# An S4D convolution by FFT: the input's 4096-point spectrum and the way back split as 128 by 32 instead of 64 by 64

## The chip, the cores and the metric

The kernel runs on one core of a Trainium2 chip. The metric is device time in microseconds (us), from start to end of one execution. The core's engines are TensorE (PE; its weight loads are listed apart as PEld), VectorE (DVE), ScalarE (ACT), GpSimd (POOL) and SyncE (SP), whose queue issues nearly all of the transfers. Matmuls read SBUF and write PSUM, which has eight banks of 2 KB per partition.

## The reference

The block takes `A_u` of 2048 tokens by 448 channels, normalizes and modulates it, convolves each channel with a kernel of length 2048 that is a sum of 256 damped complex exponentials, adds the result to the input, and puts a token-mixing MLP (2048 to 1792 to 2048 tokens) behind it.

```python
h = layernorm(x) * (1 + ca) + sa
K = 2 * Re(einsum("dn,dnl->dl", C, exp(A * dt * pos)))      # 448 channels, 2048 positions
y = irfft(rfft(h, 4096) * rfft(K, 4096))[:2048]             # linear convolution
x = x + ga * (y + h * D_skip)
h = layernorm(x) * (1 + cb) + sb
x = x + gb * (W2 gelu(W1 h^T + b1) + b2)^T                  # MLP over tokens
```

## The kernel before

**Stages.** The program has a first part (span 0 to about 390 us) that makes the convolution, and a second (to the end) with the layer norms and the MLP. The first part is one loop over steps s = 0 to 58 that generates the convolution kernel K in 28 groups of 16 channels, two steps for each group. The spectral work is laid between the steps. A "window" stands at every eighth step: it makes the magnitudes (exponentials) of the next eight steps.

**A step.** `st_phase` puts angles into PSUM by matmuls (`xe`, `xg`, line 627). `st_step` runs six ACT functions of 512 columns (lines 683 to 688), two POOL products `G` (690, 691) and four DVE products `E` (692 to 696). `st_mag2` makes a magnitude product on POOL (666, 671), in the loop for later steps below 32 and in the windows otherwise. `st_kgen` sums E times G over the exponentials on PE (`kg`, 717). `st_s1` transforms a finished pair of groups along one axis (`y`, 755, 32 matmuls of 64x64 into two PSUM tiles), and two copies put it into `yk` (761).

**The spectrum of the input.** The transform has 4096 points, split 64 by 64. `u_rows` (548; 32 calls) multiplies a quarter of the partitions (32 tokens) by a row table `wur`, which POOL makes from `wu` and the layer norm's scales (535). The result goes through `yt` to DRAM (`yu_d`). `u_cols` (580; 32 calls, k = 0 to 31) loads it as `yi`, multiplies one row by a 128x128 column table out of `s2`, and adds a constant term on DVE (587) for the 17 rows in `ones_k1`; for the other 15 rows ACT copies (589). Two rows go to `us_d` in one transfer. Rows are dealt out two or three per step in steps 8 to 16, columns two or three per step in steps 17 to 28 and one per turn in the window at step 24.

**The pieces.** 16 pairs of rows times two halves of 224 channels are 32 pieces. For each, `pc_s2` makes the spectrum of the kernel (`kx`, 820: two 128x128 matmuls of 224 columns), `pc_mul` multiplies by the input's spectrum (`z`, 828, two on DVE), `pc_inv` transforms back (`vv`, 836 and 837: four matmuls of 128x128), `pc_out` copies to `vt` (842) and stores to `v_d` (846). Pieces 0 to 15 stand inside the loop from step 33, one operation group per step, with a table of 384 KB each (`si`). Pieces 16 to 31 stand behind the loop, one after another. There `pc_swap` makes a copy of `u` with its halves exchanged (805, ACT), and `pc_tables` makes a third of the tables on POOL out of the two thirds that are loaded (811 to 813). The MLP's first part, `ln_y`, ends the way back by the 32-point table `ft` (1308).

**What sets the order.** PE, ACT, DVE and POOL run in the order in which the code calls them; results that leave PSUM are put on the lists `dve` and `act`, which are emptied in the middle of the next `st_step` and after its ACT functions, or at each turn of a window. SP's queue is ordered by hand in part of the program and elsewhere by the framework. PSUM tiles of `u_rows`, `u_cols`, `y`, `kx` and `vv` come from the pool `pms` with three banks, taken in turn; behind the loop `kx` has the pool `pxs` with four.

Of the kernel before, what the change touches and what calls it, by code (L numbers as in the profile page):

```python
# [22 lines left out]
P = 128  # L23
# [17 lines left out]

def dft_tables():
    n1 = np.arange(32)
    k1 = np.arange(32)
    n2 = np.arange(64)
    k2 = np.arange(64)
    nn = 4096
    t = {}
    w = 2 * np.pi * np.outer(n1, k1) / 64
# [9 lines left out]
    t["WU"] = np.tile(w1.transpose(1, 2, 0).reshape(32, 64), (4, 1))  # L59

    t["WC"] = wc.reshape(P, 2, 2, 2, 32).swapaxes(3, 4).reshape(P, 2 * P)
    s = np.zeros((2, 64, 32, 2, 64))
    i1 = np.zeros((2, 64, 32, 2, 64))
    i2 = np.zeros((2, 64, 32, 2, 64))

    def inverse(rows, cols, k, m, ang):
        a = np.cos(ang) * 2 / nn
        b = np.sin(ang) * 2 / nn
        i1[0, rows, k, m[0]] = a
        i1[1, rows, k, m[0]] = -b  # L70
        i2[1, rows, k, m[0]] = -a
        i2[0, rows, k, m[0]] = -b
        if len(m) > 1:
            i1[0, rows, k, m[1]] = b
            i1[1, rows, k, m[1]] = a
            i2[1, rows, k, m[1]] = -b
            i2[0, rows, k, m[1]] = a

    for k in range(1, 32):
        ang = 2 * np.pi * np.outer(n2, k + 64 * k2) / nn  # L80
        s[0, :, k, 0] = np.cos(ang)
        s[1, :, k, 0] = np.sin(ang)
        s[0, :, k, 1] = -np.sin(ang)
        s[1, :, k, 1] = np.cos(ang)
        inverse(slice(None), None, k, (0, 1), ang.T)


    for q in range(32):
        ang = 2 * np.pi * n2 * (32 + 64 * q) / nn
        s[1, :, 0, 0, q] = np.cos(ang)  # L90
        s[1, :, 0, 1, q] = -np.sin(ang)
        inverse(q, None, 0, (1,), ang)
    for q in range(33, 64):
        ang = 2 * np.pi * n2 * (64 * (q - 32)) / nn
        s[0, :, 0, 0, q] = np.cos(ang)
        s[0, :, 0, 1, q] = -np.sin(ang)
        inverse(q, None, 0, (0,), ang)
    s[0, :, 0, 0, 32] = 1
    s[0, :, 0, 1, 32] = (-1.0) ** n2
    i1[0, 32, 0, 0] = 1 / nn  # L100
    i2[1, 32, 0, 0] = (-1.0) ** n2 / nn
    s2 = s.reshape(P, 32 * P)

    t["S2"] = s.reshape(2, 4, 8, 2, 32 * P).transpose(3, 0, 2, 1, 4).reshape(P, 32 * P)

    one = np.einsum("cnk,cqkm->km", w1, s.reshape(2, 64, 32, P))
    t["SV"] = one[ones_k1()].T

    order = lambda a: a.reshape(P, 32, 2, 2, 2, 16).transpose(0, 1, 5, 2, 4, 3)
    t["I1"] = order(i1)  # L110
    t["I2"] = order(i2)
    ft = np.zeros((32, 2, 2, 32, 2))
    w = 2 * np.pi * np.outer(k1, n1) / 64
    f0 = np.cos(w)
    f1 = -np.sin(w)
    f0[0] = 1
    f1[0] = (-1.0) ** n1
    for h in range(2):
        ft[:, 0, h, :, h] = f0
        ft[:, 1, h, :, h] = f1  # L120
    t["FT"] = ft.reshape(P, 64)
    fl = np.zeros((4, 4, 2, 2, 2 * LAST, 2, 64))
    for r in range(2):
        for g in range(2):
            fl[r, :, g, r, :, g] = t["FT"].reshape(32, 4, 64)[-2 * LAST :].swapaxes(0, 1)
    t["FL"] = fl.reshape(32, 2 * 2 * LAST * P)
# [16 lines left out]

    v1, v2 = (t.pop(k).reshape(2, 64, 32, P) for k in ("I1", "I2"))
    j1 = np.stack([v1[0], v2[1]])
    j2 = np.stack([v1[1], v2[0]])
    for nm, tabs, n in (("SI", (s2, v1, v2), NP), ("SJ", (s2, j1, j2), 1), ("SK", (s2, v1), NP)):
        tabs = [a.reshape(P, NP, 2, P)[:, :n] for a in tabs]  # L150
        t[nm] = np.stack(tabs, 2).reshape(P, n * len(tabs) * 2 * P)
    return {k: np.ascontiguousarray(v.astype(np.float32)) for k, v in t.items()}


def ones_k1():

    return [0] + list(range(1, 32, 2))


def token_rows(a):  # L160

    return a.rearrange("(n g h r) d -> r g n h d", g=2, h=2, r=16)


def token_pair(a, r, g):

    rows = a.rearrange("(n g h r) d -> g n h (r d)", g=2, h=2, r=16)
    return rows[g, :, :, r * D : (r + 2) * D]


class WeightStream:
# [12 lines left out]
    def load(self):  # L184
# [4 lines left out]
        if n < 32:  # L189
            fh, r = divmod(n, 16)  # L190
            for g in range(2):
                self.nc.sync.dma_start(w[64 * g : 64 * g + 64], self.w1[r, g, :, :, fh * 896 : (fh + 1) * 896])
# [34 lines left out]
def tile_adaln_s4d_mixer(ctx, tc, i, out):  # L227
    nc = tc.nc
    x = i["A_u"][0]
    xv = x.rearrange("(n g r) d -> r g n d", g=4, r=16)  # L230
# [17 lines left out]
    with ExitStack() as es:  # L248
# [54 lines left out]
        def x_load(r0, n, eng=nc.sync):  # L303
            for g in range(4):
                to = xt[32 * g : 32 * g + 32, r0 : r0 + n, 0:D]
                (nc.sync if r0 > 7 and g < 2 else eng).dma_start(to, x.rearrange("(n g r) d -> g n r d", g=4, r=16)[g, :, r0 : r0 + n])
# [19 lines left out]
        wu = xp.tile([P, 64], F32, name="wu")  # L326
# [7 lines left out]
        svt = sp2.tile([P, 17], F32, name="svt", bufs=1)  # L334
# [197 lines left out]
        def u_table(R):  # L532
            wurs[R] = xp.tile([P, 2, 64], F32, tag="wur", name="wur", bufs=3)
# [39 lines left out]
        def u_cols(k):  # L573
# [22 lines left out]
            if k % 2 and k // 2 + 4 < 16:  # L596
                u_load(k // 2 + 4)
                if kk == 3 and n + 2 < 8:
                    s2_load(n + 2)
# [868 lines left out]
```

## Time and profile before

| | |
|---|---|
| three timed runs | 694.22, 697.17, 698.87 us; median 697.17 |
| the profiled execution | 692.88 us; span 691.1 us, mean granted clock of TensorE 0.988 |
| busy, of the span | PE 642.3, PEld 485.7, ACT 451.0, DVE 429.0, POOL 277.0 us |
| transfers | 128.15 MB in 99759 packets, mean 185 GB/s |
| from 500 us on | PE 25.0 of every 25 us, MLP only |

The profile counts the busy time of an engine as the union of its instructions. A busy sum by group (an instruction's line, its tiles, its shape) adds overlapping instructions, so PE groups add up to more than the span. One f32 matmul is two records. DMA shares are of the 16 DMA engines and go up to 1.08 where all of them are always at work.

### The profile page before, as it was taken

To read this page: it belongs to the slowest core of one execution; us is meant where nothing else is said; L and a number is where in the kernel's file an instruction comes from. 1 tells how busy PE (TensorE), PEld (TensorE's weight loads), DVE (VectorE), ACT (ScalarE), POOL (GpSimd) and SP (SyncE) were. 2 spreads that over 40 slices of the span, in tenths; PEclk is the share of its full clock that TensorE was granted. 3 is DMA by queue.
4 is the path that set the end of the run, shared out by engine and by line. 5 is a ranking of instruction groups with operands and counts; after the bars stand their busy time and mean duration, and the time that the engine had idled before them with its cause. 6 is when DMAs were issued, how large, how long until landed. Compare 5 with 4: busy or idle time off the path is not lost.

```text
span 691.1 us, 18518 instructions
## 1 busy us (share of the span) xinstructions
PE 642.3 (93%) x7322; PEld 485.7 (70%) x7322; DVE 429.0 (62%) x818; ACT 451.0 (65%) x848; POOL 277.0 (40%) x363
## 2 busy tenths in 40 slices
PE   0877999999988899999999989999999999999997
PEld 0444555445445676676789857778899999999997
DVE  7896899786665584856744578876732364444431
ACT  5788598899869799999767678887322352222220
POOL 6685588498578767777658200000000000000000
PEclk9989999999999899999999999999999999999999
DMA  7695757598876476554589799955563445555540
GB/s 180 183 204 139 241 172 239 205 253 245 242 231 168 124 171 162 143 162 122 142 266 375 227 263 246 250 151 153 180 215 113 141 133 160 160 167 168 166 125 28
DMA packets 99759, 128.15 MB, mean 185 GB/s; under 512 B 13460, under 2 KB 80440, under 8 KB 99672
## 3 DMA queue, kind: packets, MB, share of 16 engines
q1 hardware_dynamic: 98728, 124.34, 63.4%
q0 software_dynamic: 944, 2.62, 1.6%
q8 instruction: 58, 0.95, 0.6%
q14 instruction: 29, 0.24, 0.1%
HBM read 91.57 MB, written 34.87 MB: 183 GB/s over the span
## 4 chain that ended last, share of the span: by engine, by line
PE 69%; DMA 10%; ACT 8%; DVE 5%; issue 3%; POOL 2%; SPq 1%; DVEq 0%; ACTq 0%; POOLq 0%
PE o L1434 7%; PE o L1436 6%; PE o L1435 6%; PE xe L627 6%; PE acc L1271 6%; PE acc L1272 6%; PE acc L1273 5%; PE kg L717 5%; PE vv L836 3%; PE vv L837 3%; PE kx L820 3%; DMA w<-in_B_w_dram 3%; PE pu L580 3%; PE pu L548 2%; DMA wm<-in_w_mod_dram 2%
## 5 line engine op out<-in xcount | busy, mean ns | idle before, releaser
L212 ACT CAST whi<-w 128x896 fp32r<-128x896 f32 x64 | 59.7, 939 | 135.1 <-PE o L1435 82.6
L690 POOL TENSOR_TENSOR G<-mag,gs 128x512 f32<-128x512 f32 x56 | 72.0, 1286 | 52.4 <-ACT gs L686 52.4
L221 DVE TENSOR_TENSOR wlo<-w,whi 128x896 fp32r<-128x896 f32 x64 | 68.1, 1086 | 39.6 <-ACT whi L212 36.5
L1271 PE MATMUL acc<-h3h,whi 128*128 128x448 f32 x224 | 83.0, 371 | 2.0 <-ACT h3h L1344 1.1
L1272 PE MATMUL acc<-h3l,whi 128*128 128x448 f32 x224 | 81.3, 363 | 0.6 <-DVE h3l L1345 0.4
L1434 PE MATMUL o<-uh,whi 128*128 128x448 f32 x224 | 81.3, 363 | 0.0
L1436 PE MATMUL o<-uh,wlo 128*128 128x448 f32 x224 | 81.2, 362 | 0.0
L1273 PE MATMUL acc<-h3h,wlo 128*128 128x448 f32 x224 | 80.9, 361 | 0.0
L1435 PE MATMUL o<-ul,whi 128*128 128x448 f32 x224 | 80.6, 360 | 0.0
L717 PEld LDWEIGHTS kg<-E,G 128*32 128x32 f32 x3584 | 55.9, 113 | 29.3 <-issue 18.5
L691 POOL TENSOR_TENSOR G<-mag,gs 128x512 f32<-128x512 f32 x56 | 72.0, 1286 | 0.0
L717 PE MATMUL kg<-E,G 128*32 128x64 f32 x3584 | 65.2, 226 | 3.2 <-issue 2.6
L627 PE MATMUL xg<-tab,lph 64*128 64x512 f32 x112 | 62.6, 559 | 5.1 <-DVE E L696 2.0
L627 PE MATMUL xe<-tab,lph 64*128 64x512 f32 x112 | 62.4, 557 | 1.3 <-ACT gs L687 1.1
L692 DVE TENSOR_TENSOR E<-m,xe 128x512 f32<-128x512 f32 x53 | 36.4, 686 | 43.5 <-ACT xe L685 25.7
L1439 DVE TENSOR_TENSOR y<-o,x 128x448 f32<-128x448 f32 x16 | 10.0, 625 | 78.8 <-PE o L1436 78.8
L671 POOL TENSOR_TENSOR m<-mag,w 128x512 f32<-128x512 f32 x53 | 55.8, 1053 | 4.1
L1271 PEld LDWEIGHTS acc<-h3h,whi 128*128 128x128 f32 x224 | 42.0, 188 | 15.2 <-ACT h L1343 2.8
L828 DVE TENSOR_TENSOR z<-kx,u 128x448 f32<-128x448 f32 x48 | 28.4, 620 | 26.5 <-PE kx L820 26.4
L627 PE MATMUL xe<-tab,lex 64*128 64x512 f32 x56 | 28.9, 532 | 17.1 <-POOL wm L874 15.7
L1272 PEld LDWEIGHTS acc<-h3l,whi 128*128 128x128 f32 x224 | 42.0, 187 | 3.8 <-DVE h3l L1345 0.9
L1436 PEld LDWEIGHTS o<-uh,wlo 128*128 128x128 f32 x224 | 42.0, 188 | 3.4
(246 smaller groups left out, 1523.8 us busy)
## 6 DMA issues: line engine op xcount, KB each, us to landing
w<-in_B_w_dram SPq DMA_DIRECT2D x64, 224.0 KB
w<-in_B_w_dram SPq DMA_DIRECT2D x32, 448.0 KB
yu_d<-yt SPq DMA_DIRECT2D x16, 448.0 KB
yi<-yu_d SPq DMA_DIRECT2D x32, 224.0 KB
us_d<-uo SPq DMA_DIRECT2D x16, 448.0 KB
u<-us_d SPq DMA_DIRECT2D x32, 224.0 KB
v_d<-vt SPq DMA_DIRECT2D x32, 224.0 KB
vt<-v_d SPq DMA_DIRECT2D x14, 448.0 KB
```

The source lines that it names most:

```text
L212: self.nc.scalar.copy(hi, w)
L221: eng.tensor_tensor(lo, w, hi.bitcast(F32), ALU.subtract)
L627: T.matmul(out[k], lhs[r], rhs[r], start=start, stop=stop)
L690: G.tensor_tensor(Gt[:, 1], mg_, v32(sg), ALU.mult)
L691: G.tensor_tensor(Gt[:, 0], mg_, v32(cg_), ALU.mult)
L717: T.matmul(kg[32 * q : 32 * q + 32, m], Gt[:, c, d], E[:, c, d], start=h == 0 and c == 0 and m == 0, stop=h == 1 and c == 1, skip_group_ch ...
L1271: nc.tensor.matmul(acc[f], hi[:, fs], h3h[:, r], start=r == 0, stop=False)
L1272: nc.tensor.matmul(acc[f], hi[:, fs], h3l[:, r], start=False, stop=False)
L1273: nc.tensor.matmul(acc[f], lo[:, fs], h3h[:, r], start=False, stop=r == 15)
L1434: nc.tensor.matmul(o, hi[:, ks], uh[kh][:, k], start=kh == 0 and k == 0, stop=False)
L1435: nc.tensor.matmul(o, hi[:, ks], ul[kh][:, k], start=False, stop=False)
L1436: nc.tensor.matmul(o, lo[:, ks], uh[kh][:, k], start=False, stop=kh == 1 and k == 6)
```

## The change

The same 4096 bins are split as 128 by 32, so that what was one 128x128 table becomes 64x64 tables: the row transform now takes 64 tokens at once and gives 128 rows, and the column tables have 64 rows and 64 columns. Two rows of the transform lie side by side in the two halves of the array. The tokens are dealt to the partitions in another order (`token_rows`, `token_pair`, the loads of x and of `w1`, the reading of `v_d`), with packets of the same size.

- `u_rows`: one matmul of 64x128 per call instead of two of 32x64; `wu` and `wur` have 128 columns instead of 64.
- `u_cols`: 16 calls of four 64x64 matmuls into two PSUM banks instead of 32 calls of one 128x128 matmul; every output adds the constant term on DVE, none is an ACT copy; tables of half the size.
- `pc_s2`: four matmuls of 128x64 instead of two of 128x128.
- `pc_inv`: eight matmuls of 64x64 instead of four of 128x128, into two banks instead of one; for pieces 0 to 15 two copies of 224 columns each take them out, for pieces 16 to 31 one copy of both banks.
- Tables: 256 KB per piece, loaded whole for all 32; `pc_tables` is gone. `pc_swap` makes four copies of 32 partitions, two on POOL and two on ACT.
- Behind the loop `kx` uses `pms`, and `vv` has the pool `pxs` with two tiles of two banks.
- Of pieces 0 to 15 `u` is loaded by four transfers instead of two. `fl` is loaded by two of 32 partitions instead of one.

```diff
-        def u_cols(k):
-            n, kk = divmod(k, 4)
...
-            pm = pms.tile([P, D], F32, tag="ms", name="pu")
-            T.matmul(pm, s2[:, kk], yi[:, k % 2], start=True, stop=True)
...
+        def u_cols(p):
+            n, kk = divmod(2 * p, 4)
+            uo = up.tile([P, 2, 2, DC], F32, tag="uo", name="uo", bufs=4)
+            yi, s2 = yis[p], s2s[n]
+            pms_ = [pms.tile([P, D], F32, tag="ms", name="pu") for _ in range(2)]
+            for j in range(2):
+                for b in range(2):
+                    q, rows = b ^ j, slice(64 * b, 64 * b + 64)
+                    T.matmul(pms_[b][64 * q : 64 * q + 64], s2[rows, kk + j], yi[rows, j], start=True, stop=True)
...
-            (dve if k in ones_k1() else act).append(out)
+            for b in range(2):
+                dve.append(partial(out, b))
...
         def pc_swap(n):
...
-            for h in range(2):
-                S.copy(pw[n][64 * h : 64 * h + 64], pu[n][64 - 64 * h : 128 - 64 * h, 0])
-
-        def pc_tables(n):
...
-            G.tensor_copy(unlike[0:64], like[64:128])
-            G.tensor_copy(unlike[64:128], like[64:128])
-            G.tensor_scalar(like[64:128], like[0:64], -1.0, None, ALU.mult)
+            for q in range(4):
+                (G.tensor_copy if q < 2 else S.copy)(pw[n][32 * q : 32 * q + 32], pu[n][32 * (q ^ 1) : 32 * (q ^ 1) + 32, 0])
 
         def pc_s2(n):
...
-            for j in range(2):
-                T.matmul(pk[n][:, j], pl[n][:, 0, j], k1[:, j], start=True, stop=True)
+            pk[n] = pms.tile([P, 2, DC], F32, tag="ms", name="kx")
+            for b in range(2):
+                for q in range(2):
+                    T.matmul(pk[n][64 * q : 64 * q + 64, b], pl[n][:, 0, q, b], k1[:, q ^ b], start=True, stop=True)
...
         def pc_inv(n):
-            pv[n] = pms.tile([P, 2, DC], F32, tag="ms", name="vv")
+            if n < NP:
+                pv[n] = [pms.tile([P, DC], F32, tag="ms", name="vv") for _ in range(2)]
+            else:
+                pv[n] = pxs.tile([P, 2, 512], F32, tag="vv", name="vv")
+            halves_ = pv[n] if n < NP else [pv[n][:, q, 0:DC] for q in range(2)]
             w, z = pl.pop(n), pz.pop(n)
-            for j in range(2):
-                T.matmul(pv[n][:, j], w[:, 1, j], z[0][:, j], start=True, stop=False)
-                T.matmul(pv[n][:, j], w[:, 2, j], z[1][:, j], start=False, stop=True)
+            for t in range(2):
+                for b in range(2):
+                    for q in range(2):
+                        to, rows = slice(64 * (b ^ q), 64 * (b ^ q) + 64), slice(64 * q, 64 * q + 64)
+                        T.matmul(halves_[q][to], w[rows, 1, t, b], z[t][rows, b], start=t == 0, stop=t == 1)
...
-                elif s == 24 and e != 5:
+                elif s == 24 and e in (0, 2, 4, 6, 7):
                     some(u_cols, cols, 1)
...
-                some(u_cols, cols, 2 if s < 24 else 3)
+                some(u_cols, cols, 1)
```

Three places in the order of the instructions. The first is DVE in the steps 17 to 19, where the outputs `uo` of the columns stand between the E products of a step. Before:

```order
L692 TENSOR_TENSOR E<-m_2306,xe 128x16x32
L693 SCALAR_TENSOR_TENSOR E<-mag,xe 128x16x32
L587 SCALAR_TENSOR_TENSOR uo<-mod_104,svt,pu 128x2x224 x2
L695 TENSOR_TENSOR E<-mag,xg 128x16x32
L696 TENSOR_TENSOR E<-m_2306,xg 128x16x32
L692 TENSOR_TENSOR E<-m_2363,xe 128x16x32
L693 SCALAR_TENSOR_TENSOR E<-mag,xe 128x16x32
L587 SCALAR_TENSOR_TENSOR uo<-mod_104,svt,pu 128x2x224
L695 TENSOR_TENSOR E<-mag,xg 128x16x32
```

Of the change:

```order
L692 TENSOR_TENSOR E<-m_2274,xe 128x16x32
L693 SCALAR_TENSOR_TENSOR E<-mag,xe 128x16x32
L589 SCALAR_TENSOR_TENSOR uo<-mod_104,svt,pu 128x2x224 x2
L695 TENSOR_TENSOR E<-mag,xg 128x16x32
L696 TENSOR_TENSOR E<-m_2274,xg 128x16x32
L692 TENSOR_TENSOR E<-m_2331,xe 128x16x32
L693 SCALAR_TENSOR_TENSOR E<-mag,xe 128x16x32
L589 SCALAR_TENSOR_TENSOR uo<-mod_104,svt,pu 128x2x224 x2
L695 TENSOR_TENSOR E<-mag,xg 128x16x32
```

From the second of these steps on DVE has two outputs in every step where it had one, and ACT has none.

The second is PE at the end of step 38, ahead of the window at step 40: the last two of the 32 `y` matmuls, then a piece's `vv`, then the window's first exponents (`xe`, `xg`) and the next `kx`. Before:

```order
L755 MATMUL y_4397<-wc,ks 64x32x2
L755 MATMUL y_4398<-wc,ks 64x32x2
L836 MATMUL vv<-z_4390,si 128x224
L837 MATMUL vv<-z_4392,si 128x224
L836 MATMUL vv<-z_4390,si 128x224
L837 MATMUL vv<-z_4392,si 128x224
L627 MATMUL xe<-tab,lex_145 128x512
L627 MATMUL xg<-tab,lex_145 128x512
L717 MATMUL kg<-E,G 32x64 x32
L820 MATMUL kx<-yk_1228,si 128x224 x2
```

Of the change:

```order
L755 MATMUL y_4427<-wc,ks 64x32x2
L755 MATMUL y_4428<-wc,ks 64x32x2
L832 MATMUL vv<-z_4420,si 64x224 x4
L832 MATMUL vv<-z_4422,si 64x224 x4
L627 MATMUL xe<-tab,lex_145 128x512
L627 MATMUL xg<-tab,lex_145 128x512
L717 MATMUL kg<-E,G 32x64 x32
L809 MATMUL kx<-yk_1218,si 64x224 x4
```

The order is the same; `vv` is now two groups of four quadrants, the first of which already writes both of its banks. With `y` in two of the three banks of `pms`, the second bank of `vv` is one that `y` has filled.

The third is ACT at the same place: what empties these banks stands behind the six functions of step 39. Before:

```order
L687 ACTIVATE gs<-gs 128x512
L688 ACTIVATE xg<-ab 128x512
L761 COPY yk_3700<-y_4397 128x32x2x8
L761 COPY yk_3700<-y_4398 128x32x2x8
L842 COPY vt<-vv 128x448
L650 ACT_TABLE_LOAD
```

Of the change:

```order
L687 ACTIVATE gs<-gs 128x512
L688 ACTIVATE xg<-ab 128x512
L761 COPY yk_3700<-y_4427 128x32x2x8
L761 COPY yk_3700<-y_4428 128x32x2x8
L842 COPY vt<-vv 128x224 x2
L650 ACT_TABLE_LOAD
```

The copy of `vv` has become two; the order of what stands ahead of it is unchanged.

More of the change, by code (lines that the diff above doesn't have):

```diff
@@ new lines, in dft_tables @@
+    t["WU"] = np.tile(rows.reshape(64, P), (2, 1))
+    by_row = s.reshape(2, 2, 8, 2, 32, 2, 64).transpose(0, 2, 3, 1, 4, 5, 6).reshape(64, 32, 2, 64)
+    t["S2"] = by_row.transpose(2, 0, 1, 3).reshape(P, 32 * 64)
+    one = np.einsum("ihkc,cjkhm->khm", rows, s.reshape(2, 32, 32, 2, 64))
+    pair = np.arange(32) // 2 * 2
+    held = lambda q, b: pair[::2] + (q ^ b)
+    t["SV"] = np.stack([np.stack([one[held(q, b), b] for q in range(2)], 1) for b in range(2)], 1).reshape(32, P).T
+    fs = np.zeros((16, 2, 2, 2, 64))
@@ new lines, in dft_tables @@
+    for q in range(2):
+        for g in range(2):
+            fs[:, q, g] = back[pair[::2] + g, g ^ q]
+    t["FT"] = fs.reshape(P, 64)
+    fl = np.zeros((2, 32, 2, 2 * LAST, 2, 64))
+    last = fs.reshape(32, 2, 2, 64)[-2 * LAST :]
+    for g in range(2):
+        for r in range(2):
+            for c in range(2):
+                for h in range(2):
+                    fl[g, 4 * r + 2 * c + h, r, :, h] = last[:, g, c]
+    t["FL"] = fl.reshape(64, 2 * 2 * LAST * P)
+    kx = np.zeros((P, NP, 2, 2, 64))
@@ L982, in more @@
                     return
[L986 removed]
+        rows, cols, pieces = iter(range(32)), iter(range(16)), [0, 0]
         def some(f, it, n):
```

233 lines of the change are left out of this document (106 added, 127 removed).

## The prediction

> **What bounds the kernel now.** I read the page first: the engines' sums over the span of 691.1 us, and the chain of work that ended last.
>
> ```profile
> PE 642.3 (93%) x7322; PEld 485.7 (70%) x7322; DVE 429.0 (62%) x818; ACT 451.0 (65%) x848; POOL 277.0 (40%) x363
> PE 69%; DMA 10%; ACT 8%; DVE 5%; issue 3%; POOL 2%; SPq 1%; DVEq 0%; ACTq 0%; POOLq 0%
> ```
>
> TensorE (PE) carries 69% of the chain, so less matmul time looks like less time. But POOL, busy for 40% of the span, has all its work in the first 390 us, and the change touches nothing after about 395 us. So I read stage by stage, in the table of stretches (columns: stretch; length; busy time with count for PE, PEld, DVE, ACT, POOL; granted clock; DMA share; GB/s).
>
> ```profile
> 145.00:149.00 4.00, 4.00 (x80) 2.14 (x80) 4.00 (x8) 3.97 (x9) 3.84 (x6) 1.00 0.77 222
> 275.00:300.00 25.00, 24.41 (x582) 17.40 (x584) 21.21 (x35) 23.88 (x50) 18.16 (x17) 1.00 0.55 146
> 365.00:370.00 5.00, 5.00 (x29) 5.00 (x27) 2.77 (x5) 3.66 (x7) 4.44 (x10) 1.00 1.07 382
> 385.00:390.00 5.00, 5.00 (x29) 4.72 (x27) 3.08 (x5) 3.09 (x6) 0.00 (x0) 1.00 0.80 208
> 405.00:410.00 5.00, 5.00 (x25) 3.76 (x24) 3.22 (x7) 2.96 (x8) 0.00 (x0) 1.00 1.05 260
> ```
>
> Stage A (the forward columns, 140 to 205 us): PE is full, and POOL too, 3.84 of 4.00. Stage B (first 16 pieces inside the kernel-generating steps, 217 to 352 us): PE 24.41 and ACT 23.88 of 25. Stage C (last 16 pieces, 352 to 390 us): PE is full, the other engines have room, and DMA is saturated in the middle (share 1.07) at 382 GB/s, and no longer at the end (0.80). After that, in the MLP's first part, DMA is saturated too, at only 260 GB/s. A saving on PE is therefore worth its size only in C; in A and B it is worth the distance to the next engine.
>
> **What a quadrant group costs.** The chain of waits in order of time (start, length, what; one f32 matmul leaves two records):
>
> ```profile
> 72.68 0.91 PE pu L548 x8
> 89.95 1.09 PE y L755 x64
> 142.04 1.70 PE pu L580 x4
> 173.05 0.95 PE pu L580 x2
> 187.23 5.58 DMA s<-in_S_dram
> ```
>
> A full 128x128 matmul of 448 columns takes 0.95 us alone (L580, x2), and two take 1.70: 0.75 of streaming each, and 0.20 once for the turn to another shape. Four matmuls of 449 columns on 32x64 pieces of the array (L548, x8) take 0.91 together, so four tiles do run at once. 64x64 quadrants do it as well: the 64 records of L755 are 32 matmuls of 64 columns, which one after another would be 32 x 64/448 x 0.75 = 3.4 us; they took 1.09. So a column pair (before 1.70) becomes 0.95, and a piece's inverse (before 4 x 0.375 = 1.50 of streaming) becomes 0.75. The spectrum matmuls kx go from two of 128x128 to four of 128x64, side by side in twos: 0.75 as before. Streaming saved: 16 x 0.75 + 32 x 0.75 = 36 us. How much of it reaches the end is the question.
>
> The Trainium skill, "TensorE: Matmul & The Clock Gate", Part 3, "The mechanism", says that a weight load overlaps a running matmul only where their row groups differ; four quadrants have two row groups. This trace disagrees: L755 has two row groups, and 32 loads left exposed could not fit its 1.09 us. By the rule half the loads would be in the open; the mechanism and its price stand among the rivals.
>
> **The change part by part.**
>
> *Row stage.* Matmuls per output halve, their time does not (two row halves at once instead of four quarter-height tiles). The scaled table doubles to 256 columns on POOL:
>
> ```profile
> L690 POOL TENSOR_TENSOR G<-mag,gs 128x512 f32<-128x512 f32 x56 | 72.0, 1286 | 52.4 <-ACT gs L686 52.4
> L535 POOL TENSOR_TENSOR wur<-wu,rs 128x128 f32<-128x128 f32 x8 | 3.4, 435 | 4.9 <-DVE rs L527 4.9
> L755 PEld LDWEIGHTS y<-wc,ks 64*64 64x64 f32 x896 | 15.7, 141 | 5.3 <-issue 2.6 <-POOL ks L737 1.0 <-DVE yt L551 0.6
> L693 DVE SCALAR_TENSOR_TENSOR E<-mag,xe 128x512 f32<-128x512 f32 x56 | 38.1, 680 | 0.0
> L842 ACT COPY vt<-vv 128x448 f32<-128x448 f32 x30 | 16.3, 545 | 9.5 <-PE vv L837 8.3 <-ACT yk L761 1.0
> L731 ACT COPY ks<-kg 128x256 f32<-128x256 f32 x28 | 10.8, 385 | 9.8 <-PE kg L717 8.5 <-PE kg L639 1.2
> L812 POOL COPY si<-si 64x256 f32<-64x256 f32 x15 | 6.0, 401 | 0.6
> ```
>
> From 128 to 512 columns POOL grows by 851 ns, so 256 columns cost about 720, 0.28 more. Of the 8 tables the first and the three after the window stand where POOL paces: **+1.1 us** (0 to +2.3).
>
> *Columns, steps 17 to 23.* One step of stage A, in the timeline:
>
> ```profile
> 144.81 0.26 POOL L666 TENSOR_TENSOR w<-mag 128x16 f32<-128x16 f32 x1
> 148.64 0.25 POOL L666 TENSOR_TENSOR w<-mag 128x16 f32<-128x16 f32 x1
> 145.81 1.78 PE L580 MATMUL pu<-yi,s 128*128 128x448 f32 x4
> 149.66 1.77 PE L580 MATMUL pu<-yi,s 128*128 128x448 f32 x4
> 145.85 1.26 DVE L587 SCALAR_TENSOR_TENSOR uo<-mod,svt,pu 128x448 f32<-128x448 f32 x2
> ```
>
> POOL repeats after 3.83 us and PE after 3.85. With 0.75 off PE, POOL is late next: **0**. All 32 column outputs go to VectorE (DVE), 0.63 each: with four E products of 0.68 that is 4.0 per step by durations. They overlap at their ends (two outputs together take 1.26), so I take about 3.7; POOL's 3.83 hides it, with little left.
>
> *Window 24 and steps 24 to 31.* In the window 7 groups of 0.95 become 5, 1.9 off PE; but 10 outputs instead of about 4 go to DVE, 3.8 more, in front of the parameter chain that stands there: I take **-0.7** (0 to -1.9). Steps 24 to 28 had three columns each, and a 5.58 us wait for a column table (above), of which half the bytes are left. POOL's first G product of the steps 24, 27 and 31:
>
> ```profile
> 184.36 1.28 POOL L690 TENSOR_TENSOR G<-mag,gs 128x512 f32<-128x512 f32 x1 [3.65 <-ACT gs L686]
> 199.90 1.29 POOL L690 TENSOR_TENSOR G<-mag,gs 128x512 f32<-128x512 f32 x1 [4.13 <-ACT gs L686]
> 215.52 1.30 POOL L690 TENSOR_TENSOR G<-mag,gs 128x512 f32<-128x512 f32 x1
> ```
>
> That is 31.2 us for seven steps; at POOL's own pace 7 x 3.83 = 26.8. Of the 4.4 in reach I take **-3.5** (-1 to -4.4), since the transfers of that stretch are dense. The smaller first piece table gives **-0.3** (0 to -1).
>
> *Stage B.* Two steps (kx in one, vv in the other) and the place where y stands ahead of vv:
>
> ```profile
> 285.90 1.02 PE L820 MATMUL kx<-yk,si 128*128 128x224 f32 x4
> 292.96 1.02 PE L820 MATMUL kx<-yk,si 128*128 128x224 f32 x4
> 296.07 1.26 PE L755 MATMUL y<-wc,ks 64*64 64x64 f32 x64
> 297.26 0.65 PE L836 MATMUL vv<-z,si 128*128 128x224 f32 x2
> 299.47 1.10 ACT L761 COPY yk<-y 128x512 f32<-128x512 f32 x2
> ```
>
> 7.06 us per two steps. PE would do them in 6.3; ACT was busy 23.88 of 25, so it allows 6.74, and its output becomes two copies of 224 columns instead of one of 448 (545 and 385 ns for 448 and 256 columns: two of 224 are about 0.72, in the pipelined stream some 0.1 more). So about 0.45 per plain double step, 6 of them: -2.7. Against it: vv takes two of the three PSUM banks of its pool, and after y (two banks) the second vv bank is one that y fills. vv must wait for the yk copy, at 299.47 + 0.55 = 300.0 instead of starting at 297.26. Behind it on PE stand the exponents of the next window, kernel spectra and the next kx; on ACT, after yk, the vt copy and then the window. Before, yk and vt ended at 299.47 + 1.10 + 0.5 = 301.1; now vv ends at 301.0 and two copies at 301.8. So the window starts about 0.8 late, two times: +1.6. B: **-1.1** (-2.7 to +3.4).
>
> *End of B.* Kernel spectra are done and the pieces alternate kx, z, vv on PE:
>
> ```profile
> 345.37 0.92 PE L820 MATMUL kx<-yk,si 128*128 128x224 f32 x4
> 348.78 0.92 PE L820 MATMUL kx<-yk,si 128*128 128x224 f32 x4
> ```
>
> 3.41 per piece becomes 2.66, three times -0.75 = -2.2; the third y place just ahead stalls PE by the 2.7 less the 0.75 that vv saves, about 1.8 after what ACT hides. **-0.4** (-2.2 to +1.5).
>
> *Stage C.* The first two kx stand together; then one piece in steady state, and the first work behind the last piece:
>
> ```profile
> 352.62 1.68 PE L820 MATMUL kx<-yk,si 128*128 128x224 f32 x8
> 361.11 0.92 PE L820 MATMUL kx<-yk,si 128*128 128x224 f32 x4
> 363.38 0.92 PE L820 MATMUL kx<-yk,si 128*128 128x224 f32 x4
> 361.31 0.53 ACT L842 COPY vt<-vv 128x448 f32<-128x448 f32 x1 [0.57 <-PE vv L837]
> 361.87 1.14 ACT L805 COPY sw<-u 64x448 f32<-64x448 f32 x2
> 389.95 0.60 PE L1308 MATMUL y<-vt,ft 128*64 128x224 f32 x4
> ```
>
> 2.27 per piece, 37.3 in all. Now kx (128x64 tiles) and vv (64x64) alternate in shape, so each pays the turn: 0.95 + 0.95 = 1.90 against 2.27, 16 times -0.37 = -5.9. ACT needs 0.53 + 1.14 and gaps, 1.70, as before; POOL loses three table instructions and gets two swap copies of at most 0.75 each (0.401 for 256 columns), below 1.9. DMA is the nearest limit: a piece moves 256 KB of tables and 224 KB each of u and v, 0.72 MB; at 382 GB/s that is 1.89 us. I take **-5.0** (-1 to -7).
>
> *Sum:* 1.1 - 0.7 - 3.5 - 0.3 - 1.1 - 0.4 - 5.0 = **-9.9 us**. The profiled execution took 692.88; 683.0 after. The median of the three runs before, 697.17, is 4.29 above it, so for a median I expect **687**.
>
> **The rivals.**
>
> *Another engine ends it (24%).* POOL in A, ACT in B and DMA in C take over fully: C gives -2, steps 24 to 31 -1, B +1, the row stage +1.1: about -1, **696**. For it: POOL's 3.83 and ACT's 23.88; DMA at 1.07. Against it: DMA was filling ahead there, as its share falls to 0.80 at the end of C. The Trainium skill, "TensorEngine Tiling (Array Packing)", "PSUM Bottleneck", warns of this, that emptying PSUM becomes the limit when matmuls get faster; in B the trace agrees by ACT's 23.88, in C it does not by ACT's 3.66 of 5.
>
> *Banks (12%), slower.* Three PSUM banks for pairs: a vv or a column pair waits for a copy that ACT or DVE does only behind a step's other work. If the full 2.7 us is lost at three y places (8 instead of 3.4) and each of 16 pairs waits for one DVE output (0.63) on the path, that is +4.6 + 10; with the rest of the sum **702**. It decides from 0.6 us per pair. Against it: in A POOL's pace covers such waits.
>
> *Everything lands (15%).* All the far ends: -1.9 - 4.4 - 1 - 2.7 - 2.2 - 7 + 1: about **679**.
>
> *Quadrants do not overlap their weights (4%).* Each of a vv's four rounds shows one load, 0.14 by L755's row: +0.56 per vv. C then takes 2.46 per piece, +3.0 in all; the gains of A are gone, the stalls of B (+1.6, +1.8) and the row stage's +1.1 stay, with the small table's -0.3: +7.2, about **704**. L755's 1.09 speaks against.
>
> **How the numbers follow.** Forecast 45%, the rivals as given. The forecast's own spread is 681 to 692; the range reaches to 679 and, for the takeover and half of the bank case, to **699**. A measurement tells about 1% (7 us) from no change. Faster by over 1% (below 690): 0.55, from most of the forecast and the full landing; within 1%: 0.33; slower: 0.12, from banks and weights, less what of them ends within 1%.
>
> **What would show it.** Right: column groups of 8 records in 0.95; POOL's L666 still 3.83 apart in steps 17 to 23; no table wait in steps 24 to 28; PE waiting 2.7 us ahead of vv after y; kx to kx 1.9 in C. Wrong: kx to kx at 2.2 or more with DVE or ACT waiting for transfers; PE waiting for uo outputs in A with POOL idle; a later start of the MLP's matmuls relative to the last piece, which the sum puts at none.

## The result and the profile after

The changed kernel took 694.73 us (median of 12 runs, 690.71 to 698.75), the kernel before 694.31 us on the same chip: a ratio of 0.9999, with a 95% interval of 0.9971 to 1.0027. In a second comparison it was 696.04 against 692.83 us, 1.005 (1.0027 to 1.0074). Disturbed runs are left out of the ratios, so a ratio can differ a little from that of the medians. So the change brings no gain, where -9.9 us were forecast: no difference that the first comparison can tell, some 3 us lost in the second. The base of the forecast, 697.17 us from three runs, was itself 3 to 5 us above the four later medians of the kernel before (692.2 to 694.4); the ratios are what counts here.

The page of the changed kernel, its engines' sums and the chain of work that ended last:

```profile
PE 628.4 (91%) x7706; PEld 452.3 (65%) x7706; DVE 438.7 (63%) x835; ACT 446.6 (64%) x847; POOL 269.7 (39%) x349
PE 62%; ACT 12%; POOL 8%; DMA 6%; DVE 5%; issue 5%; SPq 1%; DVEq 0%; POOLq 0%; ACTq 0%
```

TensorE's busy time fell by 14 us, not by the 36 of streaming that the change takes away, and ScalarE (ACT) has a larger part of the chain, 12% instead of 8%. The table of stretches, columns as in the prediction, shows where a part of the other 22 went: look at the granted clock, the third figure from the end. (By the clock's records TensorE was busy for 42.9 us at half clock, 17.1 in the kernel before; about half of the difference, some 13 us, is time that full clock would have saved.)

```profile
275.00:300.00 25.00, 20.91 (x556) 13.23 (x554) 21.20 (x35) 24.14 (x53) 18.25 (x16) 1.00 0.48 139
340.00:345.00 5.00, 2.50 (x64) 1.47 (x55) 4.14 (x7) 4.02 (x9) 3.56 (x3) 0.78 0.34 95
345.00:350.00 5.00, 5.00 (x131) 3.63 (x132) 1.04 (x2) 0.59 (x2) 0.00 (x0) 0.54 0.33 98
365.00:370.00 5.00, 5.00 (x72) 2.56 (x68) 2.93 (x5) 2.42 (x5) 2.54 (x5) 1.00 0.99 265
370.00:375.00 5.00, 3.25 (x36) 1.57 (x30) 2.40 (x4) 3.31 (x6) 2.20 (x4) 0.85 1.06 383
```

In plain stage B (275 to 300) TensorE now idles 4 of 25 us and ScalarE is full. From 340 to 345 TensorE is idle for half the time, and from 345 to 350 it works at 0.54 of its clock; the kernel before had 1.00 in all these stretches. In stage C a gap for transfers opens at 370 us.

The stages in us, from the starts of POOL's first G product (L690) of a step, and from the last y, the last vv, the first MLP matmul (acc from h3h) and the first matmul of o; two profiles of the changed kernel:

| stretch | before | changed | forecast of the difference |
|---|---|---|---|
| start to step 8 | 89.5 | 92.1, 91.7 | row stage: +1.1 |
| step 8 to 16 | 49.1 | 49.5, 49.4 | (in the +1.1) |
| step 16 to 23 | 25.5 | 25.5, 25.5 | 0 |
| window 24 | 20.3 | 20.5, 20.1 | -0.7 |
| step 24 to 31 | 31.2 | 26.9, 26.5 | -3.5 |
| window 32 | 16.0 | 15.8, 14.2 | -0.3 |
| steps 32 to 39, 40 to 47, 48 to 55, together | 76.2 | 75.2, 73.8 | -2.7 |
| window 40 | 16.2 | 18.3, 19.7 | +0.8 |
| window 48 | 16.2 | 18.4, 19.7 | +0.8 |
| end of B (step 55 to the end of the last y) | 10.7 | 13.9, 12.5 | -0.4 |
| stage C (to the end of the last vv) | 39.2 | 35.8, 37.0 | -5.0 |
| to the first MLP matmul | 9.5 | 12.6, 13.3 | 0 |
| to the first matmul of o | 153.2 | 150.7, 150.6 | 0 |

Stage A did in sum what was forecast, stage C 2.2 to 3.4 of 5.0 us. The windows 40 and 48 and the end of B lost 7 to 9 us where the forecast had 1.2. The MLP's start took back 3 to 4 us, of which 2.5 came back by the first matmul of o. This is the place of the last loss of B in the changed kernel, TensorE's timeline (start, length, line, operation, what ended the idle time before):

```profile
339.52 1.16 PE L755 MATMUL y<-wc,ks 64*64 64x64 f32 x64
340.52 0.56 PE L832 MATMUL vv<-z,si 64*64 64x224 f32 x2
343.59 1.76 PE L832 MATMUL vv<-z,si 64*64 64x224 f32 x14 [2.50 <-ACT yk L761]
345.28 1.93 PE L717 MATMUL kg<-E,G 128*32 128x64 f32 x64
347.15 1.76 PE L809 MATMUL kx<-yk,si 128*64 128x224 f32 x8
...
350.22 0.99 PE L832 MATMUL vv<-z,si 64*64 64x224 f32 x16
```

The wait is the predicted one: 2.5 us for the yk copy, since vv's second bank is one that y filled. What was not predicted stands behind it: vv takes 1.76 instead of 0.99 us, the kernel spectrum kg 1.93 instead of 1.10, kx 1.76. TensorE runs at half speed. Laid along the edges of the recorded clock, the table of stretches says when that happens:

```profile
254.12:257.53 3.41, 1.29 (x50) 0.75 (x42) 2.98 (x6) 3.41 (x8) 2.14 (x3) 0.99 0.58 159
257.53:260.95 3.42, 3.23 (x48) 1.88 (x52) 0.94 (x2) 2.03 (x5) 1.20 (x1) 0.51 0.16 29
298.40:301.80 3.40, 1.24 (x16) 0.69 (x16) 2.71 (x5) 2.81 (x7) 2.50 (x2) 1.00 0.54 153
301.80:305.20 3.40, 3.40 (x74) 2.46 (x72) 0.00 (x0) 2.75 (x5) 0.96 (x2) 0.51 0.48 145
```

Each time a stretch of 3.41 us in which TensorE was busy for 1.2 to 1.3 us is followed by one at 0.51 of the clock. The records of the granted clock have three stretches at half clock after 60 us in the kernel before (193, 224 and 234 us) and ten in the changed kernel: at 70, 186, 223, 234, 257, 302, 343 (two), 374 and 397 us.

### The profile page after: what moved, and what is told of

The parts are those of the page before. It is cut to its first block, busy times and chain, and to the rows that moved or that the text cites. A ratio compares the mean times of both kernels' runs of the same rounds, so it can differ in the third digit from the quotient of the medians.

```text
span 693.5 us, 19319 instructions
## 1 busy us (share of the span) xinstructions
PE 628.4 (91%) x7706; PEld 452.3 (65%) x7706; DVE 438.7 (63%) x835; ACT 446.6 (64%) x847; POOL 269.7 (39%) x349
## 4 chain that ended last, share of the span: by engine, by line
PE 62%; ACT 12%; POOL 8%; DMA 6%; DVE 5%; issue 5%; SPq 1%; DVEq 0%; POOLq 0%; ACTq 0%
PE o L1434 7%; PE acc L1270 6%; PE o L1433 6%; PE o L1435 6%; PE acc L1271 6%; PE acc L1272 6%; PE xe L627 5%; PE kg L717 4%; POOL G L691 3%; POOL G L690 2%; PE xg L627 2%; PE vv L832 2%; PE kx L809 2%; PE kg L639 2%; PE y L1307 2%
## 5 line engine op out<-in xcount | busy, mean ns | idle before, releaser
L690 POOL TENSOR_TENSOR G<-mag,gs 128x512 f32<-128x512 f32 x56 | 71.8, 1282 | 46.0 <-ACT gs L686 45.9
L717 PEld LDWEIGHTS kg<-E,G 128*32 128x32 f32 x3584 | 58.1, 117 | 31.7 <-issue 22.1
L717 PE MATMUL kg<-E,G 128*32 128x64 f32 x3584 | 68.2, 231 | 4.1 <-issue 4.1
L692 DVE TENSOR_TENSOR E<-m,xe 128x512 f32<-128x512 f32 x53 | 36.3, 684 | 35.2 <-ACT xe L685 25.1
L832 PE MATMUL vv<-z,si 64*64 64x224 f32 x512 | 36.8, 385 | 9.4 <-ACT yk L761 6.2
L627 PE MATMUL xe<-tab,lex 64*128 64x512 f32 x56 | 31.0, 569 | 15.7 <-POOL wm L874 14.8
L1433 PEld LDWEIGHTS o<-uh,whi 128*128 128x128 f32 x224 | 42.1, 188 | 3.4
```

The lines of the kernel that those rows point to most:

```text
L627: T.matmul(out[k], lhs[r], rhs[r], start=start, stop=stop)
L690: G.tensor_tensor(Gt[:, 1], mg_, v32(sg), ALU.mult)
L717: T.matmul(kg[32 * q : 32 * q + 32, m], Gt[:, c, d], E[:, c, d], start=h == 0 and c == 0 and m == 0, stop=h == 1 and c == 1, skip_group_ch ...
L1433: nc.tensor.matmul(o, hi[:, ks], uh[kh][:, k], start=kh == 0 and k == 0, stop=False)
```

## The experiments

Two things had to be told apart at the y places: the wait itself, and the half clock behind it; and in stage C, which of its transfers holds it. The theories carry letters in the expectations: A, the wait (with or without the clock) is the loss; B, ScalarE sets the pace anyway; C, the half clock is the larger part; D, transfers hold stage C; E, its engines do; F and G, chance or the row stage for what was lost ahead of step 8; H and I, the reload of v or other work for the MLP's start.

### vv moved behind other work

```diff
-            if s > 32:
+            if s > 32 and (free or s % 2 or s >= NHALF):
                 piece(pieces[0] < NP and (s % 2 == 1 or s >= NHALF))
```

`free` says that the step has no y. A step without `piece` leaves its vv to the next one.

> The changed kernel, but in the three even steps 38, 46 and 54, where y stands ahead of a piece's vv, the vv comes one step later, behind the next kernel spectrum and exponents; nothing else is changed, and nothing is left out. Theory A (the wait of vv for y's copy, which the two PSUM banks of vv bring, and the stretch at half clock that follows each of them, cost what stage B lost): the waits of 2.5 to 3.0 us ahead of vv at 255, 299 and 341 us shrink to under 1 us, the half clock stretches at 258, 302 and 343 to 350 us are gone, the windows 40 and 48 take 16.3 instead of 18.3 us, the end of B is 3 us shorter: -4 to -7 us, some 689 us. Theory B (ScalarE sets the end of B's steps anyway, and the wait on TensorE is its shadow): within 1 us of the changed kernel, 694 to 695 us, the windows 40 and 48 stay at 18 us.

687.95 us, 0.9925 of the time before (0.9898 to 0.9952), 8.1 us less than the changed kernel in the same comparison. Windows 40 and 48 take 16.1 us, the end of B 10.1. ScalarE and TensorE at window 40, to be held against the changed kernel's ScalarE below it:

```profile
250.97 0.62 ACT L688 ACTIVATE xg<-ab 128x512 f32<-128x512 f32 x1
251.49 1.10 ACT L761 COPY yk<-y 128x512 f32<-128x512 f32 x2
...
252.37 0.99 PE L832 MATMUL vv<-z,si 64*64 64x224 f32 x16
...
252.61 1.28 ACT L650 ACT_TABLE_LOAD   x1
253.90 0.60 ACT L650 ACTIVATE mag<-xe 128x512 f32<-128x512 f32 x1
```

```profile
256.53 0.62 ACT L688 ACTIVATE xg<-ab 128x512 f32<-128x512 f32 x1
257.05 1.10 ACT L761 COPY yk<-y 128x512 f32<-128x512 f32 x2
259.53 0.59 ACT L842 COPY vt<-vv 128x224 f32<-128x224 f32 x2 [1.38 <-PE vv L832]
260.14 1.28 ACT L650 ACT_TABLE_LOAD   x1
261.43 0.60 ACT L650 ACTIVATE mag<-xe 128x512 f32<-128x512 f32 x1
```

In the changed kernel vv stands between two pieces of ScalarE's work: it waits for yk, and the window's first exponential waits for vt. From the step's last sine to that exponential it is 4.90 us; with the shift 2.93. A holds (it claimed -4 to -7; by the ratios the shift is worth 5 us against the first comparison of the changed kernel and 9 against the second); B falls. The shift takes away the wait and the half clock together, so it doesn't tell them apart.

### The second bank alone, in the kernel before

```diff
+            if n < NP:
+                pv[n] = [pms.tile([P, DC], F32, tag="ms", name="vv") for _ in range(2)]
...
-                copy(vt, from_)
+                for q in range(2):
+                    copy(vt[:, q], from_[q])
```

> The kernel before, unaltered but for one thing: in the first 16 pieces vv's two halves of 224 columns lie in two PSUM banks instead of one (and are copied by two copies of 224 columns, as in the changed kernel); its matmuls, tables and transfers stay. Theory A (the second bank alone, through vv's wait for y's copy, costs what stage B lost): waits of 2 to 3 us ahead of vv in the steps 38, 46 and 54, half clock behind them, windows 40 and 48 at 18 to 20 us instead of 16.2, the end of B 3 us longer: 6 to 10 us slower than the kernel before, 699 to 703 us. Theory B (the wait is covered by ScalarE, and the loss comes from the 64x64 matmuls themselves): within 1.5 us of the kernel before.

697.90 us, 1.008 of the time before (1.005 to 1.0111), by the ratio some 5.6 us. Windows 18.5 and 18.6, the end of B 12.5. TensorE at window 40:

```profile
254.53 1.16 PE L755 MATMUL y<-wc,ks 64*64 64x64 f32 x64
255.62 0.65 PE L840 MATMUL vv<-z,si 128*128 128x224 f32 x2
...
258.60 1.11 PE L840 MATMUL vv<-z,si 128*128 128x224 f32 x2 [1.95 <-ACT yk L761]
```

With full 128x128 matmuls and the old tables, one bank more for vv costs 6.5 us in the two windows and the end of B, against 7.5 and 8.8 in the two profiles of the changed kernel. Half clock follows in both windows (1.11 us instead of 0.65), not at the third place, where the 1.8 us are lost without it. By the ratio the time came out just under A's 6 to 10 us. The quadrants are not needed for the loss. The second copy came along with the bank; the shifted kernel has it too, and its windows take 16.1 us.

### TensorE kept busy in the wait

```diff
             if s > 32:
+                if not free and s % 2 == 0 and s < NHALF:
+                    warm(20)
```

> The changed kernel with 20 idle matmuls (bf16, 256 columns, 0.11 us each, 2.1 us together) put between y and vv in the steps 38, 46 and 54; their result is not used. The wait of vv for y's copy stays, but TensorE is busy in it. Theory C (the clock is halved for the 3.41 us that follow a stretch of 3.41 us in which TensorE was busy for half the time or less; the wait itself is mostly hidden, the half clock behind it is what costs): the granted clock stays at 1.00 from 250 to 350 us, vv behind the wait takes 1.0 instead of 1.76 us, the windows 40 and 48 gain 0.8 to 1.5 us each and the end of B about 2.8: -3 to -5 us, some 691 us. Theory A (the wait itself costs): the clock stays up but the time comes down by at most 1 us. If the idle matmuls outlast the wait: up to 1 us slower at each of the three places.

692.82 us, 1.0006 (0.9981 to 1.0031), and 3.2 us less than the changed kernel beside it, as theory C has it; the granted clock stayed at 1.00 from 250 to 350 us. But the idle matmuls ended about 1 us after the bank was free, and the windows stayed at 17.9 and 18.2 us. So the same with 10 of them:

```diff
-                    warm(20)
+                    warm(10)
```

> The changed kernel with 10 instead of 20 idle matmuls between y and vv in the steps 38, 46 and 54 (1.1 us, which should fit into the wait; the 20 took 2.36 us and ended 0.9 us after the bank was free). Their result is not used. Theory C (of what stage B lost, the wait itself is the smaller part, about the 0.8 us per place that the prediction gave it, and the half clock behind it the larger): the clock stays at 1.00 from 250 to 310 us, vv behind the wait takes 1.0 instead of 1.76 us, the windows 40 and 48 take 17.0 us (16.1 in the shifted kernel, 17.9 and 18.2 with 20 idle matmuls, 18.3 to 19.7 in the changed kernel); 4 to 5 us less than the changed kernel, 0.996 of the time before. Theory A (the wait itself is the larger part): the windows stay at 18 us and the time within 0.5 us of that with 20 idle matmuls, 1.000.

691.02 us, 0.9972 (0.9952 to 0.9993). The windows took 16.9 and 17.0 us, the end of B 11.1. The stretches around the wait at window 40, and TensorE's timeline in it:

```profile
253.10:256.50 3.40, 1.97 (x72) 1.71 (x71) 3.04 (x6) 3.32 (x8) 2.14 (x3) 1.00 0.55 145
256.50:259.90 3.40, 3.40 (x92) 2.38 (x92) 1.28 (x2) 2.79 (x6) 1.63 (x2) 1.00 0.38 83
```

```profile
255.89 1.27 PE L639 MATMUL kg<-ones 128*128 128x256 bf16 x10
257.08 1.01 PE L832 MATMUL vv<-z,si 64*64 64x224 f32 x16
```

Busy for 1.97 instead of 1.29 us of the stretch, TensorE keeps its clock, and vv takes 1.01 us. This splits the loss of a window (18.3 to 19.7 us, against 16.1 without the wait): 0.8 us is the wait, 1.3 to 2.8 the half clock. Theory C holds for the windows. What it is worth in time is less sure: 0.9972 is 2 us below the first comparison of the changed kernel (0.9999, intervals that overlap) and 5 below the second (1.005, intervals that don't), and the changed kernel didn't run beside these runs. Nor did the idle matmuls keep the clock everywhere: one stretch at half clock stands at 318 us, behind window 48, where the plain steps took 76.7 us in all instead of 73.8 and 75.2.

### Stage C: half the tables, and one buffer more for u

```diff
-                    if m < 2 * NP:
+                    if m < 2 * NP and (m % 2 == 0 or m == 19):
                         pc_w(m, swp if (m - NP) % 6 in (4, 5) else None)
+                        if m > 19:
+                            pl[m + 1] = pl[m]
```

> The changed kernel with half of the piece tables of the last 12 pieces left out: pieces 21, 23 to 31 use the table of the piece before, so 6 transfers of 256 KB fewer between 355 and 385 us (the output is then not the layer's). Theory D (stage C and the start of the MLP are held by the transfers: 1.67 us wait for a table at 370 us, the half clock stretches at 374 and 398, and the wait of 1.65 us for v at 394): the table wait is gone, kx to kx is 1.82 us from start to end, the last vv ends 3 to 4 us earlier relative to the start of C, the MLP starts 1 to 3 us earlier still: -4 to -7 us. Theory E (a compute engine's pace or the copies hold stage C): within 1 us of the changed kernel.

691.98 us, 1.000 (0.9981 to 1.0019), 4.1 us less than the changed kernel beside it. That is the lower end of what D expected. Its profile doesn't show where: kx no longer waits for a table, but stage C took 35.2 us (35.8 to 37.0 in the five profiles that have the same code in stage C), the MLP's start 13.1, and the profiled spans are 692.4 and 692.6 us. The profiled execution here was 2.2 us slower than its run's median and that of the changed kernel 1.7 faster, so this pair of profiles says little; E is not borne out by the time, and the tables are not cleared. In all these profiles GpSimd and ScalarE wait in stage C mostly for u, whose buffer comes free late. So one buffer more, on the shifted kernel:

```diff
-            u = fp.tile([P, 2, 2, DC], F32, tag="u", name="u", bufs=3)
+            u = fp.tile([P, 2, 2, DC], F32, tag="u", name="u", bufs=4)
...
-                if k % 2 == 0 and n + 4 < 2 * NP:
-                    pc_u(n + 4)
+                for m in (n + 4, n + 6) if k == 0 else (n + 6,) if k % 2 == 0 else ():
+                    if m < 2 * NP:
+                        pc_u(m)
```

> The shifted kernel of the first experiment, with four instead of three buffers for pairs of u, and each pair of the last 16 pieces asked for two pieces earlier. Theory D1 (stage C waits for u because its buffer comes free late: 13 us of waits of GpSimd's swap copies for u, at 5 to 6 us per transfer): the waits for u fall to some 3 us and the stretch from the last y to the last vv from 36.8 to 33 to 35 us, -1 to -3 us in all, unless the MLP's start gives it back. Theory D2 (the transfers' rate as a whole holds it, DMA share 1.06 at 385 GB/s): the waits move from u to the tables, the stretch stays within 0.7 us.

684.74 us, 0.9886 of the time before (0.9844 to 0.9929): faster than both kernels, and the best of this case. The waits of stage C by line (engine, line, for what; sum, times, longest), first in the shifted kernel, then here:

```profile
POOL sw L801 <- DMA u<-us_d: 13.1, 6, 2.7
```

```profile
POOL sw L801 <- DMA u<-us_d: 7.9, 2, 7.1
```

Of the 7.9, one wait of 7.1 stands at the start of the stage; D1 had some 3 in all. Stage C took 35.1 us (36.8 with the shift alone, 35.8 to 37.0 without the buffer), the MLP's start 10.7 (13.2). So the waits for u went as D1 has it, the stage came out at the far end of its 33 to 35 us, and the gain shows more in the MLP's start than in the stage. D2 isn't cleared: kx still waits 2.0 us for tables (2.4 before), and the transfers' share from 360 to 375 us is 1.06 at 381 to 386 GB/s. The interval overlaps that of the shift alone (0.9898 to 0.9952), so the size of this part rests on the profiles. The same edit without the shift:

> The changed kernel with the fourth buffer for pairs of u and the earlier request alone, without the shift of vv. If what stage C and the start of the MLP lost is a matter of u's buffers, whatever happens in stage B: the stretch from the last y to the first MLP matmul takes 45 to 47 us (45.8 with the shift, 48.4 and 50.3 in the two profiles of the changed kernel), 2 to 4 us less than the changed kernel, 0.997 of the time before. If it worked only because the shifted stage B leaves other work to the transfers: 48 to 50 us, and the changed kernel's time, 1.000 to 1.005.

693.43 us, 0.9998 (0.9964 to 1.0031). The stretch from the last y to the first MLP matmul took 46.1 us, as expected (48.4 and 50.3 without the edit); windows and end of B stayed at 18.4, 18.5 and 13.9 us. From there to the first matmul of o it took 152.4 us (150.7 and 150.6), so some 1.7 us of this gain were given back. By the time the two readings aren't told apart: 0.997 lies in the interval, and so does 1.000.

### The start of the MLP

On the shifted kernel, with one piece more handed over on the chip (vt keeps its four buffers):

```diff
-LAST = 3
+LAST = 4
```

> The shifted kernel of the first experiment, with the last four pieces instead of three handed to the MLP's first two row blocks straight from on-chip memory, so that the reload of v from DRAM waits for piece 27 instead of 28. Theory H (the 13 us from the last vv to the first MLP matmul, 9.5 in the kernel before, are the chain of a store of 3.35 and a reload of 3.68 us, which three pieces at 2.27 us covered and three at 1.9 don't): the reload's wait of 2.2 us goes, the last vv to the first MLP matmul takes 11 to 12 us: -1 to -2 us against the shifted kernel's 0.9925 of the time before. Theory I (the weights' transfers or VectorE hold the MLP's start): no gain, up to 1 us slower, by the four matmuls more of about 0.45 us.

689.30 us, 0.9943 (0.9912 to 0.9975), not better than the shift alone. The reload's wait ahead of L1313 went from 2.21 us (1.65 in the changed kernel) to 0.68, as H says, but the next reload took its place:

```profile
389.46 0.60 PE L1313 MATMUL y<-vt,ft 96*64 96x224 f32 x4 [0.68 <-DMA vt<-v_d]
...
398.11 0.97 PE L1307 MATMUL acc<-vt,ft 128*64 128x448 f32 x4 [2.12 <-DMA vt<-v_d]
```

and the matmuls that replace the reload (L1301, 12 records in 2.54 instead of 8 in 1.78 us) cost 0.8 twice. The start stayed at 13.2 us. With this edit and the fourth buffer for u together:

> The two edits before together. If C is held by u's buffers and the MLP's start by the reload of v, the gains add: -2 to -5 us against the shifted kernel, 0.986 to 0.990 of the time before. If the start of the MLP is held by one common limit (all transfers between 340 and 400 us), the stretch from the last y to the first MLP matmul stays at 49 to 50 us, as in the kernels so far (48.3 to 50.3), and the time is the shifted kernel's.

684.93 us, 0.9887 (0.9846 to 0.9928): what the buffer for u gives alone. The gains don't add. The stretch from the last y to the first MLP matmul took 47.8 us, between the two theories and longer than with the buffer alone (45.7). With the buffer alone the reload's wait ahead of that line had already fallen to 1.14 us; that the reload is late because stage C's transfers are is therefore likely, not shown.

### The changed kernel again

> The changed kernel once more, unaltered, for a second profile beside the others. Theory F (the half clock stretches before 75 us, at 53 and 70 us, hang on where the 3.41 us grid of the clock falls against the same idle times, so they are chance): in this profile and the other three of this call, whose first 250 us are the same code, the start of step 8 differs by 1 to 3 us from profile to profile and some of them have no half clock at 53 or 70. Theory G (the row stage with its doubled tables brings them): step 8 starts 2.5 us later than in the kernel before in all four. The time is that of the changed kernel, 694 to 695 us.

696.04 us. In the ten profiles with the changed kernel's first 250 us, step 8 starts between 89.4 and 92.7 us, 91.4 on average; in the two with the old ones at 89.5 and 90.8. Most of the 2.6 us by which the changed kernel was late at step 8 is therefore chance (F), about 1.2 may be the row stage. Half clock at 53 us appears in a profile of each kind.

## Why the prediction was wrong, step by step

The first profile of the changed kernel is 2.4 us longer than that of the kernel before, 12.3 more than the forecast's -9.9. Of these, the windows 40 and 48 and the end of B make 6.3, the start up to step 16 makes 1.9, stage B's plain steps 1.7, stage C 1.6, window 24 makes 0.9 and the MLP 0.6; steps 24 to 31 gave 0.8 more than forecast.

*Row stage, +1.1.* Not contradicted. The doubled table (wur, L540) took 612 ns against 400, not 720 against 435; steps 8 to 16 lost 0.3 to 0.4 us in every profile. The 1.2 us at the start can't be told from its scatter of 3.3 us.

*Steps 17 to 23, 0.* Right: POOL's w product (L666) repeats after 3.8 us as before,

```profile
147.84 0.24 POOL L666 TENSOR_TENSOR w<-mag 128x16 f32<-128x16 f32 x1
...
151.65 0.24 POOL L666 TENSOR_TENSOR w<-mag 128x16 f32<-128x16 f32 x1
...
170.76 0.98 PE L585 MATMUL pu<-yi,s 64*64 64x448 f32 x8
```

and a column pair takes 0.98 us where nothing holds it. Five of the seven pairs of these steps took 1.5 us and more; POOL's pace hides that.

*Window 24, -0.7.* It gave nothing (20.5 and 20.1 against 20.3), the end of that term's range at 0. That the column outputs in front of VectorE's parameter chain ate the gain is likely, not shown. The smaller first table's -0.3 can't be seen beside window 32's 15.8 and 14.2 us.

*Steps 24 to 31, -3.5.* Right, and a little more: G of steps 24, 27 and 31 now start at

```profile
187.53 1.27 POOL L690 TENSOR_TENSOR G<-mag,gs 128x512 f32<-128x512 f32 x1
...
200.32 1.28 POOL L690 TENSOR_TENSOR G<-mag,gs 128x512 f32<-128x512 f32 x1 [0.29 <-ACT gs L686]
...
214.38 1.27 POOL L690 TENSOR_TENSOR G<-mag,gs 128x512 f32<-128x512 f32 x1
```

26.9 us for seven steps, POOL's own pace.

*Stage B, -1.1, and its end, -0.4.* Here the prediction failed, in the sentences "So the window starts about 0.8 late, two times" and "the third y place just ahead stalls PE by ... about 1.8 after what ACT hides". The wait, its cause and even its sizes were right: with the clock kept up, the windows lost 0.8 us each and the stretch from step 55 to the last kernel spectrum 1.7 (5.4 against 3.7 us). But both were worked out at full clock, and the wait itself took the clock away: 2.1 to 3.5 us per window, 3.1 to 4.5 at that spectrum. The three alternating pieces gave 1.3 of their 2.2 us, the plain double steps 1.0 and 2.4 of 2.7. There the prediction's own figures allowed less than it took: ScalarE's 6.74 and 0.1 for the second copy leave about 0.2 us of the 7.06 per double step, 1.3 in six, not 0.45 and 2.7; ScalarE is now busy for 24.14 of 25 us.

*Stage C, -5.0.* The mechanism was right where data was there, and the pitch of 1.90 nearly:

```profile
366.59 0.98 PE L809 MATMUL kx<-yk,si 128*64 128x224 f32 x8
...
368.41 0.98 PE L809 MATMUL kx<-yk,si 128*64 128x224 f32 x8
...
371.98 0.98 PE L809 MATMUL kx<-yk,si 128*64 128x224 f32 x8 [1.67 <-DMA si<-in_SJ_dram]
...
395.63 0.60 PE L1313 MATMUL y<-vt,ft 104*64 104x224 f32 x4 [1.65 <-DMA vt<-v_d]
```

1.82 us from kx to kx, and then a wait for transfers. Over the stage a piece took 35.8/16 = 2.24 us, the sign that the prediction had named against itself (2.2 or more, with waits for transfers), and the stage gave 2.2 to 3.4 us. The step that failed is the pitch: 1.90 us was compared with a piece's bytes at 382 GB/s, 1.89, as if each transfer were there in time. Both u and the tables were late. In the shifted kernel's chain from 340 to 395 us the tables have 23.3% and u 21.2%, with 5.3 to 6.4 us for a transfer of u. A fourth buffer for u took the stage to 35.0 and 35.1 us, half the tables to 35.2, all from 35.8 to 37.0. What holds the rest above 16 times 1.82 us stays open.

*"A later start of the MLP's matmuls relative to the last piece, which the sum puts at none."* It was 3 to 4 us later: a reload that pieces of 2.27 us had covered now waits 1.65 to 2.2 us, and half clock follows (at 397 us in the changed kernel). Of this, some is given back: from the last vv to the first matmul of o the changed kernel takes 163.3 and 163.9 us, the kernel before 162.7.

Of the rivals, "another engine ends it" came nearest in time, about -1 us, but by luck: it had C about right at -2, while steps 24 to 31 gave 4.3 us instead of its 1, and the windows and the end of B, which it put at +1 with the rest of B, lost 7 to 9. It also read ScalarE's 23.88 us as the emptying of PSUM: only some 4 of them are copies (vt, ks, yk), the rest are the steps' six functions. "Banks" came nearest in place: the y waits at full price are what happened, but not by the wait's 2.7 us. No rival had the clock, though its half clock stretches stood in the records of the kernel before (193, 224 and 234 us), one of them behind the table wait that the prediction quoted.

## What to carry to other kernels

When TensorE gets faster, look for the places where it will then wait for about half of a 3.4 us stretch or more, and price the work behind them at half clock; the best remedy here was to move other work in between. Before a tile takes a second PSUM bank, count the banks at every place where another user of the pool stands ahead of it: one bank more cost 5.6 us here without any change to the arithmetic. And a stage whose pieces follow each other faster needs its buffers counted by the time of a transfer as well as by rate (5 to 6 us here against 1.8 us per piece). With the shift and the fourth buffer the change went from no gain to 0.9886, the shift alone being worth 0.9925.

## What the runs showed of the hardware

The granted clock of TensorE changes on a fixed grid of 3.413 us and takes the values 1.0 and 0.5. In all twelve profiles, cut along that grid between 30 and 680 us, 39 stretches had TensorE busy for less than 45%, by the profile's matmul times: all 39 were followed by half clock, and in only five of them did TensorE do nothing at all. Of 49 between 45 and 60% 29 were followed by half clock, of 2184 above 60% 24 were; 16 of these 24 were at half clock themselves, where the same work takes nearly twice the busy time (vv 1.76 instead of 0.99 us). Four of the other eight were 90% busy, at 218 to 220 us; they stay unexplained. So it isn't idleness alone: a stretch that is a third busy is enough. The Trainium skill, "TensorE: Matmul & The Clock Gate", Part 1, states the free-running window of 3413 ns and the half rate, which the records here bear out; it gives an idle window as the cause of half rate, which is narrower than what these runs show.

A stretch of half clock costs what of its 1.7 us stands on the path: 1.3 to 2.8 us per window here, the more where two such stretches followed each other. Where the grid lies against the kernel's waits differs from run to run (the same wait at window 40 gave one half clock stretch in one profile, two in another). That this is why the runs of one kernel scatter over some 10 us is likely, but no run here shows it.
